# Two exponential buffers, pre-added sums from the sixth pair on, and a new order for an attention and gated-layer kernel

## The chip, the cores and the metric

The kernel runs on one core of a Trainium2 chip. Its time is microseconds of device time for one execution; the number compared is the median of several runs. Engines are named as the profile names them: PE (TensorE, matrix products), DVE (VectorE), ACT (ScalarE), POOL (GpSimd), SP (SyncE, which issues most DMAs). PEld is PE's weight load.

## What is computed

Causal attention with a bias from a running sum, then a gated layer, all in float32, on 8 batches of 8 heads, 576 positions and head size 64; the gated layer has width 1024.

```python
scores = scale * np.matmul(q, k.transpose(0, 1, 3, 2))
causal = np.triu(np.ones((S, S), dtype=bool), k=1)
s_pos = np.maximum(s, 0.0)
cum = np.cumsum(s_pos, axis=-1)
bias = -(cum[:, :, :, None] - cum[:, :, None, :])
scores = np.where(causal, -1000000000.0, scores + np.minimum(bias, 0.0))
scores = scores - np.max(scores, axis=-1, keepdims=True)
attn = np.exp(scores)
attn = attn / (np.sum(attn, axis=-1, keepdims=True) + 1e-09)
x = np.matmul(attn, v)           # then heads side by side: (B, S, 512)
...
h = np.maximum(x @ w_in, 0.0)
for k in range(3):               # along positions, zero padded
    conv_out += conv_w[k][None, None, :] * hp[:, k:k + S, :]
gate = 1.0 / (1.0 + np.exp(-conv_out))
return (h * gate @ w_out).astype(np.float32)
```

## The kernel before

**Work.** The 64 heads are 32 pairs; pair `p` holds two heads of batch `p // 4` on the two halves of the 128 partitions. Products are made to float32 accuracy from high and low parts (three products for one). Each pair goes through these steps (names in quotes are the task names in the code):

- "qk", "v": DMAs bring K, Q and V. "hi", "lo" split K and Q.
- "sh", "mx", "tn", "rt", "ds": rough scores on PE and their row maxima on DVE, turned and sent by DMA into a row that shifts the scores.
- "sc" (L1215 to L1234): the scores on PE, keys on partitions, four PSUM parts per pair. Pairs below `B0 = 9` get their causal mask as extra products from the tiles `mrow` and `unit`; later pairs get it on POOL ("mk", L1257).
- "ex" (L1248): ACT writes the exponentials into the tile `pt`, which holds both heads. There is one such tile, so a pair's exponentials come after the last reader of the pair before.
- "ad" (L1296): from pair 9 on, four additions fold the five key blocks of `pt` into the tile `ad` (all but the first 128 columns). Each may run on DVE or on POOL. The mask tiles `mrow` and `unit` lie in the memory of `ad`, so the first additions wait for the last mask products ("last_mask").
- "sum" (L1311): PE sums the exponentials over the keys, with `onehot` as weights; 28 products of a pair without additions, 10 with them. "pv" (L1273): PE multiplies the exponentials by V.
- "gd", "fo", "inv", "ri", "rb": ACT copies the sums, SP folds them over partitions (`rc`), DVE takes reciprocals (L1365), SP stores them in DRAM (L1370) and spreads them over the partitions of the one tile `rb` (L1380). "vn" copies the value product to `vc`, "nm" multiplies in place in `rb`, "xh" and "xl" (L1409, L1413) write the high and low parts of x in two position halves, into rings `x0` of 6 and `x1` of 8 slots.

A batch whose four pairs are done goes through the gated layer in two position halves: "h" (L1440, PE, groups of 24 products for two blocks of w_in), ACT's relu, the three taps on DVE and ACT, the sigmoid on ACT, the gate product on DVE, its high and low parts into ring `u`, and "o" (L1591, PE, groups of 12). Early on the weights are unpacked on ACT, POOL and DVE through staging tiles; the narrow pieces of w_out go through the tiles `ht` and `ct`.

**Order.** The order on each engine is fixed when the program is built. `Sched.play` is a planner: each task has the engines it may run on, a cost, the tasks and buffers it needs, and a due time from its place (`at(p)`, `h_tag`), shifted by a number of the table `DUE` for its kind and pair. It plays the program and always takes the ready task that is due first. Where PE has nothing ready for 0.6 us it puts in a fill product (`stay_awake`, L1668). The order it finds is then written out, and each engine runs its own list in that order, with semaphores for the true dependences.

Of the kernel before, what the change touches and what calls it, by code (L numbers as in the profile page):

```python
# [31 lines left out]
NX = (6, 8)  # L32
# [45 lines left out]
B0 = 9  # L78
RB = 7
# [16 lines left out]
    "pads":  # L96
        "0 -135.98 1 -136.71 2 -132.38",
    "ind":
# [398 lines left out]
def kernel(  # L497
# [91 lines left out]
    if RB < NP:  # L589
        EK_t.append(ep.tile([P, FW], F32R, name="eke"))  # L590
# [331 lines left out]
    for ch in range(2):  # L922
        for f in range(NF):
# [16 lines left out]
            if wide:  # L940
                t_wo[f, 1] = t_wo[f, 0]
                staged.append(t_wo[f, 0])
# [803 lines left out]
```

## Time and profile before

| | us |
|---|---|
| runs | 757.16, 758.41, 758.78 |
| median | 758.41 |
| profiled execution, its own time | 753.07 |
| its span, first to last instruction | 751.3 |
| mean granted TensorE clock in the span | 1.000 |

The profile has one row per instruction with start and duration. "Busy" is the time in which an engine has at least one instruction in work. A row of the timeline joins instructions of one line on one engine that follow each other; `x48` is their number. A product of float32 stands as two records where it is one row in the order with a count. Windows give busy time in a stretch of the span. Pairs are counted from 0, so the sixth pair is pair 5.

### The profile page before, as it was taken

What the parts mean: (1) busy time and instruction counts of PE and PEld (TensorE: products, weight loads), DVE (VectorE), ACT (ScalarE), POOL (GpSimd) and SP (SyncE); (2) the same over time, 40 slices, a digit from 0 to 9 for tenths busy, and PEclk for the clock granted to TensorE, in tenths of its full rate; (3) what the DMA queues carried; (4) which work ended last, traced back from release to release, by engine and by line L of the source; (5) the groups of instructions that cost most, each with busy time, mean ns of one, the idle gap of its engine ahead of it and who ended that gap; (6) DMA issues with size and microseconds to landing.
All of it is one profiled execution on the core that took longest, in us unless ns stands there. A gap on an engine that the chain in (4) does not pass through costs nothing.

```text
span 751.3 us, 24363 instructions
## 1 busy us (share of the span) xinstructions
PE 730.9 (97%) x10052; PEld 616.2 (82%) x10052; DVE 536.1 (71%) x1404; ACT 392.1 (52%) x676; POOL 335.2 (45%) x466
## 2 busy tenths in 40 slices
PE   8999999999999999999999999999999999999999
PEld 6777798888889887788887888887878877888897
DVE  7898987676888458678777468776856758655642
ACT  6557656365654346553646446474654436623531
POOL 6684445314436447544342547534664733410000
PEclk9999999999999999999999999999999999999999
DMA  7765631532323333342323433234222432010001
GB/s 224 222 193 156 200 100 38 161 102 83 114 72 93 115 97 102 102 126 68 97 69 112 130 116 99 83 93 152 83 68 64 135 102 64 19 43 20 29 30 44
DMA packets 50089, 75.50 MB, mean 100 GB/s; under 512 B 13690, under 2 KB 26298, under 8 KB 49978
## 3 DMA queue, kind: packets, MB, share of 16 engines
q1 hardware_dynamic: 49960, 73.92, 32.6%
q8 instruction: 79, 1.29, 0.7%
q14 instruction: 32, 0.26, 0.1%
q10 hardware_dynamic: 18, 0.02, 0.0%
HBM read 63.53 MB, written 10.03 MB: 98 GB/s over the span
## 4 chain that ended last, share of the span: by engine, by line
PE 45%; DVE 9%; issue 3%; ACT 2%; POOL 2%; DMA 1%; POOLq 0%; ACTq 0%; DVEq 0%; SPq 0%
PE ps L1448 15%; PE ps L1602 15%; PE ps L1232 7%; PE ps L1283 5%; DVE ps L1145 3%; DVE ct L1502 2%; PE ps L1335 1%; PE ps L1108 1%; DVE r L1145 1%; DVE ct L1523 1%; PE ps L1668 1%; DMA rw<-cum_d 1%; DVE ct L1486 1%; ACT pt L1249 0%; POOL ad L1298 0%
## 5 line engine op out<-in xcount | busy, mean ns | idle before, releaser
L1448 PE MATMUL ps<-x,wi 64*128 64x258 f32 (+1 forms) x3072 | 227.1, 297 | 5.4 <-DVE ct L1523 3.9
L1448 PEld LDWEIGHTS ps<-x,wi 64*128 64x128 f32 x3072 | 212.5, 186 | 12.5 <-DVE ct L1523 5.5
L1602 PE MATMUL ps<-wo,u 64*128 64x512 f32 x1536 | 196.9, 394 | 0.9
L1602 PEld LDWEIGHTS ps<-wo,u 64*128 64x128 f32 x1536 | 140.3, 185 | 28.7 <-ACTq L813 3.2
L1145 DVE CUSTOM_DVE_ANT_0 ps<-ps,rw 128x448 f32<-128x448 f32 (+4 forms) x250 | 109.5, 439 | 46.1 <-POOL rw L1066 17.4
L1249 ACT ACTIVATE pt<-ps,less 128x1024 f32<-128x1024 f32 (+1 forms) x128 | 116.1, 928 | 41.8 <-PE ps L1232 36.1
L1502 DVE SCALAR_TENSOR_TENSOR ct<-ps,cw_sb,ct 128x255 f32<-128x255 f32 (+3 forms) x256 | 115.9, 507 | 2.8 <-ACT ct L1484 2.7
L1232 PE MATMUL ps<-s 64*128 64x288 f32 (+4 forms) x1152 | 106.8, 299 | 2.8 <-DVE ct L1523 1.3
L1066 POOL TENSOR_SCALAR_AFFINE_SELECT rw<-rw 128x256 f32<-128x256 f32 (+1 forms) x125 | 47.7, 390 | 111.9 <-DVE r L1145 43.6
L1283 PE MATMUL ps<-pt,v 128*32 128x448 f32 (+4 forms) x1536 | 92.8, 388 | 0.0
L1232 PEld LDWEIGHTS ps<-s 64*128 64x128 f32 (+1 forms) x1152 | 81.1, 177 | 9.3 <-ACT pt L1249 2.6
L1283 PEld LDWEIGHTS ps<-pt,v 128*32 128x32 f32 x1536 | 50.6, 110 | 39.8 <-issue 29.9
L1260 POOL TENSOR_SCALAR_AFFINE_SELECT pt<-pt 128x256 f32<-128x256 f32 (+1 forms) x115 | 42.8, 390 | 88.9 <-ACT pt L1249 60.4
L1469 ACT ACTIVATE ps<-ps 128x642 f32<-128x642 f32 (+1 forms) x64 | 40.8, 637 | 71.5 <-PE ps L1448 67.9
L1517 ACT ACTIVATE ct<-ct 128x640 f32<-128x640 f32 (+1 forms) x64 | 43.8, 685 | 62.3 <-DVE ct L1502 59.4
L1523 DVE TENSOR_TENSOR ct<-ct,ps 128x640 f32<-128x640 f32 (+1 forms) x64 | 48.0, 751 | 18.6 <-ACT ct L1517 18.5
L1537 POOL TENSOR_TENSOR u<-ct,u 128x512 fp32r<-128x512 f32 x32 | 41.3, 1290 | 44.4 <-ACT u L1532 39.7
L1486 DVE TENSOR_SCALAR ct<-ps,cw_sb 128x256 f32<-128x256 f32 (+1 forms) x52 | 26.1, 513 | 47.6 <-ACT ct L1484 39.8
L1413 POOL TENSOR_TENSOR x<-rb,x 128x322 fp32r<-128x322 f32 (+1 forms) x50 | 37.7, 776 | 47.1 <-ACT x L1409 43.0
L1108 PE MATMUL ps<-s 64*128 64x288 f32 (+4 forms) x384 | 47.8, 307 | 5.2 <-ACT pt L1249 1.6
L1532 ACT CAST u<-ct 128x512 fp32r<-128x512 f32 x59 | 36.5, 618 | 25.8 <-DVE ct L1523 24.4
L1232 PE MATMUL ps<-eq,ek 64*128 64x288 f32 (+1 forms) x360 | 49.8, 297 | 0.0
(121 smaller groups left out, 980.2 us busy)
## 6 DMA issues: line engine op xcount, KB each, us to landing
raw<-qk SPq DMA_DIRECT2D x32, 576.0 KB
rw<-cum_d SPq DMA_DIRECT2D x25, 576.0 KB
v<-vp SPq DMA_DIRECT2D x32, 320.0 KB
rb<-ri_d SPq DMA_DIRECT2D x64, 144.0 KB
out<-ob SPq DMA_DIRECT2D x32, 256.0 KB
w<-w_in SPq DMA_DIRECT2D x8, 512.0 KB
ht<-w_out SPq DMA_DIRECT2D x8, 256.0 KB
w<-w_out SPq DMA_DIRECT2D x4, 512.0 KB
```

Of the source, the lines that this page charges most:

```text
L1066: nc.gpsimd.affine_select(out=RW_t[:, :, o : o + k], in_=RW_t[:, :, d : d + k], pattern=[[0, 2], [-1, k]], compare_op=ALU.is_ge, fill=NEG, ...
L1108: nc.tensor.matmul(dst[j], l, m, start=(k == 0), stop=(k == 1 or late))
L1145: nc.vector.tensor_tensor_reduce(out=bank(pb, j, o, o + c1 - c0), in0=bank(pb, j, o, o + c1 - c0), in1=add_, scale=1.0, scalar=acc if c0 e ...
L1232: nc.tensor.matmul(d, l, m, start=(k < 2), stop=(k >= len(steps) - 2 or (t == L and k < 2)), skip_group_check=t == L,)
L1249: nc.scalar.activation(PT[:, :, o : o + w], both(pb, 0, w), AF.Sigmoid, bias=less, scale=0.125,)
L1260: nc.gpsimd.affine_select(out=reg, in_=reg, pattern=[[0, 2], [1, dg]], compare_op=ALU.is_ge, fill=0.0, base=0, channel_multiplier=-1,)
L1283: nc.tensor.matmul(bank(pvs, n, o0, o0 + c1 - c0)[gs], vt[0:jt, t, gs], PT_t[g // 2][0:jt, O_T[t] + c0 : O_T[t] + c1], start=(t == 0), sto ...
L1448: mm = nc.tensor.matmul(bank(hb, i, 0, XW[hf]), wi[rows[j], k_ // 2, c, f * P : f * P + P], x[rows[j]], start=not turned and k == 0, stop= ...
L1502: nc.vector.scalar_tensor_tensor(cc[:, lo:hi], h_[:, sh + lo : sh + hi], cw_sb[:, 3 * f + k : 3 * f + k + 1], cc[:, lo:hi], op0=ALU.mult, ...
L1517: nc.scalar.activation(cc, cc, AF.Sigmoid)
L1523: nc.vector.tensor_tensor(cc, cc, both(hb, 2 * hf, 2 * hf + hw), op=ALU.mult)
L1602: mm = nc.tensor.matmul(bank(pb2 if m else pb, m, 0, cw_), l, r, start=turned + fp + n == 0, stop=turned == 1 and fp == FP - 1 and n == le ...
```

## The change

There are two tiles `pt`; each holds both heads of a pair and is given to a pair as a whole. Additions on `ad` start at pair 5 (`AD0`) instead of 9 (`B0`, which still rules the masks), so pairs 5 to 8 make ten sum products instead of 28 and sixteen additions more are made. `mrow` and `unit` have tiles of their own, and the first additions no longer wait for the last mask products. To make room, `x1` has 6 slots instead of 8, `rt` one instead of two, and the staging tiles `ht` lie in the memory that is given up when the gated layer's tiles are opened; all pieces of w_out (`staged`) and `cw` must be done before that. All numbers of `DUE` are new, so every engine's order is new.

```diff
-NX = (6, 8)
+NX = (6, 6)
...
 B0 = 9
+AD0 = 5
 RB = 7
...
-        "s -485.52 clear -169.14 ident -54.42 tab 40.83 hot -2.04 unit 129.42 mrow 278 "
+        "s -447.43 clear -126.39 ident -67.62 tab 470.29 hot 614.44 unit 108.55 mrow -399.5 "
...
-    PT = const.tile([P, 2, sum(W_T)], F32, name="pt")
-    PT_t = [PT[:, j] for j in range(2)]
+    PT_t = [const.tile([P, 2, sum(W_T)], F32, name=f"pt{i}") for i in range(NPT)]
...
-    mrow = ad_t.bitcast(BF16).rearrange("p a c -> p (a c)")[:, 0 : 4 * P].rearrange(
-        "p (k i m) -> p k i m", k=2, i=2
-    )
-    unit = ad_t.bitcast(BF16).rearrange("p a c -> p (a c)")[:, 4 * P : 4 * P + D]
+    mrow = const.tile([P, 2, 2, P], BF16, name="mrow")
+    unit = const.tile([P, D], BF16, name="unit")
...
-    RT_t = [const.tile([2 * NT, P], F32R, name=f"rt{i}") for i in range(2)]
+    RT_t = [const.tile([2 * NT, P], F32R, name=f"rt{i}") for i in range(1)]
...
-    H_t = [const.tile([P, 2, XW[0]], F32, name=f"ht{i}") for i in range(NHT)]
...
+    H_t = [ep.tile([P, 4 * P], F32, name=f"ht{i}") for i in range(NHT)]
...
-                staged.append(t_wo[f, 0])
+            staged.append(t_wo[f, ch])
...
-        ad = buf("ad") if p >= B0 else None
+        ad = buf("ad") if p >= AD0 else None
...
                     tt_on(e)(
-                        acc, PT[:, :, P:S] if t == 1 else acc,
-                        PT[:, :, O_T[t] : O_T[t] + W_T[t]], op=ALU.add,
+                        acc, PT_t[pts[0].slot][:, :, P:S] if t == 1 else acc,
+                        PT_t[pts[0].slot][:, :, O_T[t] : O_T[t] + W_T[t]], op=ALU.add,
                     )
...
-                    [m for t_, m in masks if t_ in (t - (t == 1), t)] + [t_ad] + last_mask, A + 2, pre_add,
+                    [m for t_, m in masks if t_ in (t - (t == 1), t)] + [t_ad], A + 2, pre_add,
...
-    stage_left = set(t_wi.values()) | set(staged) | set(last_sh)
+    stage_left = {t_cw} | set(t_wi.values()) | set(staged) | set(last_sh)
```

The order on PE, first eight of the fourteen rows of pair 5's sums before (`ps` is PSUM; the columns of a product stand last):

```order
L1335 MATMUL ps_64<-pt,onehot 32x144 x8
L1335 MATMUL ps_64<-pt,onehot 32x16
L1335 MATMUL ps_64<-pt,onehot 32x144 x3
L1335 MATMUL ps_64<-pt,onehot 32x16
L1335 MATMUL ps_64<-pt,onehot 32x144 x3
L1335 MATMUL ps_64<-pt,onehot 32x32
L1335 MATMUL ps_64<-pt,onehot 32x144 x2
L1335 MATMUL ps_64<-pt,onehot 32x32
```

The same place in the new order, the second head's sums and the value product behind them:

```order
L1336 MATMUL ps_66<-pt_89,onehot 32x128
L1336 MATMUL ps_66<-ad,onehot 32x16
L1336 MATMUL ps_66<-ad,onehot 32x144 x3
L1284 MATMUL ps_66<-pt_89,v_87 32x128 x4
L1284 MATMUL ps_66<-pt_89,v_87 32x448 x8
L1284 MATMUL ps_66<-pt_89,v_87 32x320 x4
L1284 MATMUL ps_66<-pt_89,v_87 32x192 x4
L1284 MATMUL ps_66<-pt_89,v_87 32x64 x4
```

Three rows, five products, stand for each head; the exponentials come from the second of the two `pt` tiles, and most columns from `ad`.

PE behind the last pair's value product (its last row is the first one here), before; `x_90` is the ring `x1`, L1448 the hidden layer, L1602 the output:

```order
L1283 MATMUL ps_65<-pt,v_87 32x64 x4
L1448 MATMUL ps_64<-x_90,wi 128x258 x24
L1448 MATMUL ps_65<-x_90,wi 128x258 x24
L1602 MATMUL ps_66<-wo,u_1699 128x512 x12
L1448 MATMUL ps_65<-x_90,wi 128x258 x24
L1602 MATMUL ps_66<-wo,u_1700 128x512 x12
L1448 MATMUL ps_64<-x_90,wi 128x258 x24
L1602 MATMUL ps_66<-wo,u_1701 128x512 x12
```

And in the new order, where `x_91` is the ring `x1`:

```order
L1284 MATMUL ps_67<-pt_88,v_87 32x64 x4
L1449 MATMUL ps_64<-x_91,wi 128x258 x24
L1603 MATMUL ps_65<-wo,u_1777 128x512 x12
L1449 MATMUL ps_64<-x_91,wi 128x258 x24
L1603 MATMUL ps_65<-wo,u_1778 128x512 x12
L1603 MATMUL ps_65<-wo,u_1779 128x512 x12
L1669 LDWEIGHTS mask
L1669 MATMUL ps_66<-mask 128x256
```

Two hidden-layer groups, both of batch 6, are left instead of five with 258 columns; behind the last row shown follow 22 more fill products, two output groups and then the first products that need x of pair 31.

DVE in the same place, from the copy of the last pair's value product on, before:

```order
L1389 COPY vc<-ps_65 128x128
L1389 COPY vc<-ps_65 128x448
L1486 TENSOR_SCALAR ct_103<-ps_64,cw_sb 128x256
L1502 SCALAR_TENSOR_TENSOR ct_103<-ps_64,cw_sb,ct_103 128x256 x2
L1365 RECIPROCAL rc<-rc 128x9
L1502 SCALAR_TENSOR_TENSOR ct_103<-ps_64,cw_sb,ct_103 128x255 x2
L1523 TENSOR_TENSOR ct_103<-ct_103,ps_64 128x2x256
```

And in the new order:

```order
L1390 COPY vc<-ps_67 128x128
L1390 COPY vc<-ps_67 128x448
L1366 RECIPROCAL rc<-rc 128x9
L1410 CAST x_90<-rb 128x322
L1410 CAST x_91<-rb 128x258
L1414 TENSOR_TENSOR x_90<-rb,x_90 128x322
L1414 TENSOR_TENSOR x_91<-rb,x_91 128x258
L1503 SCALAR_TENSOR_TENSOR ct_102<-ps_64,cw_sb,ct_102 128x256 x2
L1503 SCALAR_TENSOR_TENSOR ct_102<-ps_64,cw_sb,ct_102 128x255 x2
L1524 TENSOR_TENSOR ct_102<-ct_102,ps_64 128x2x256
L1538 TENSOR_TENSOR u_1775<-ct_102,u_1775 128x512
L1393 TENSOR_TENSOR rb<-vc,rb 128x576
```

The casts and subtractions of x of pair 30 now stand behind pair 31's reciprocal; before they stood ahead of the first row shown (the casts on ACT).

## Rows read from the trace of the kernel before

**Rows 1.** The page's busy times: us (share of the span) xinstructions, by engine.

```profile
PE 730.9 (97%) x10052; PEld 616.2 (82%) x10052; DVE 536.1 (71%) x1404; ACT 392.1 (52%) x676; POOL 335.2 (45%) x466
```

**Rows 2.** Windows of four stretches: length, busy time by engine, PEclk, DMA share, GB/s.

```profile
0.00:108.00 108.00, 102.58 (x1580) 81.25 (x1582) 94.06 (x203) 67.15 (x118) 65.36 (x71) 1.00 0.64 188
108.00:250.00 142.00, 139.73 (x2028) 121.71 (x2026) 106.11 (x298) 74.43 (x126) 57.17 (x82) 1.00 0.31 95
250.00:666.00 416.00, 405.47 (x5487) 340.95 (x5487) 293.47 (x816) 219.34 (x378) 209.43 (x310) 1.00 0.31 94
666.00:752.00 86.00, 83.16 (x973) 72.33 (x965) 42.50 (x88) 31.22 (x55) 3.24 (x4) 1.00 0.10 33
```

**Rows 3.** The same windows for the fill products of L1668 alone.

```profile
0.00:108.00 108.00, 23.85 (x164) 16.19 (x164) 1.00 0.64 188
250.00:666.00 416.00, 3.03 (x23) 2.01 (x23) 1.00 0.31 94
666.00:752.00 86.00, 5.17 (x41) 3.69 (x41) 1.00 0.10 33
```

**Rows 4.** PE's timeline, sums and value product of pairs 4 and 9: start, us, what.

```profile
84.08 1.77 PE L1335 MATMUL ps<-pt,onehot 128*32 128x144 f32 x54
85.72 2.87 PE L1283 MATMUL ps<-pt,v 128*32 128x128 f32 x46
...
192.81 0.30 PE L1335 MATMUL ps<-pt,onehot 128*32 128x128 f32 x1
193.38 2.87 PE L1283 MATMUL ps<-pt,v 128*32 128x128 f32 x48
```

**Rows 5.** Tile ad: ns min/median/max, first and last start; then L1413 from the lines.

```profile
L1298 POOL TENSOR_TENSOR ad<-ad,pt x37: 448/1007/1570, 187.9 to 660.2; 128x128 f32<-128x128 f32 x15, 128x384 f32<-128x384 f32 x13, 128x640 f32<-128x640 f32 x9
L1298 DVE TENSOR_TENSOR ad<-ad,pt x32: 278/573/2356, 205.8 to 661.3; 128x640 f32<-128x640 f32 x14, 128x384 f32<-128x384 f32 x10, 128x128 f32<-128x128 f32 x8
L1298 POOL TENSOR_TENSOR ad<-pt x16: 2102/2118/2128, 179.0 to 637.1; 128x896 f32<-128x896 f32 x16
L1298 DVE TENSOR_TENSOR ad<-pt x7: 1079/1086/1150, 203.0 to 656.5; 128x896 f32<-128x896 f32 x7
...
L1413 DVE TENSOR_TENSOR x<-rb,x 128x322 fp32r<-128x322 f32 (+1 forms) x14 | 7.1, 545 | 1.4 <-PE ps L1448 1.1 <-ACT x L1409 0.2
```

**Rows 6.** PE's timeline, the sums of pairs 19 and 20 and their value products.

```profile
421.37 0.30 PE L1335 MATMUL ps<-pt,onehot 128*32 128x128 f32 x1
422.66 2.87 PE L1283 MATMUL ps<-pt,v 128*32 128x128 f32 x48
...
437.59 0.30 PE L1335 MATMUL ps<-pt,onehot 128*32 128x128 f32 x1
...
439.25 2.87 PE L1283 MATMUL ps<-pt,v 128*32 128x128 f32 x48
```

**Rows 7.** Timelines of PE, SP and POOL behind the last pair's value product.

```profile
666.48 3.18 PE L1448 MATMUL ps<-x,wi 64*128 64x258 f32 x48
670.86 1.63 PE L1448 MATMUL ps<-x,wi 64*128 64x258 f32 x24
672.32 1.55 PE L1602 MATMUL ps<-wo,u 64*128 64x512 f32 x12
673.69 1.62 PE L1448 MATMUL ps<-x,wi 64*128 64x258 f32 x24
...
672.31 1.17 SPq L1380 DMA_DIRECT2D rb<-ri_d  x2
...
679.62 1.49 POOL L1413 TENSOR_TENSOR x<-rb,x 128x322 fp32r<-128x322 f32 x2 [18.40 <-ACT x L1409]
```

**Rows 8.** POOL's timeline, the low part of x of pair 20.

```profile
466.27 1.49 POOL L1413 TENSOR_TENSOR x<-rb,x 128x322 fp32r<-128x322 f32 x2 [2.98 <-DVE rc L1365]
```

**Rows 9.** Tile wo, the staging's last step on POOL: ns min/median/max, first and last start.

```profile
L934 POOL TENSOR_TENSOR wo<-ct,wo x5: 733/739/831, 66.9 to 105.8; 128x256 fp32r<-128x256 f32 x5
```

More of the change, by code (lines that the diff above doesn't have):

```diff
@@ L91 @@
     "x":
[4 rows of a table removed]
[4 rows of a table added]
     "pads":
-        "0 -135.98 1 -136.71 2 -132.38",
+        "0 35.97 1 144.1 2 512.86",
     "ind":
[1 row of a table removed]
[1 row of a table added]
     "cw":
[1 row of a table removed]
[1 row of a table added]
     "wi":
[3 rows of a table removed]
[3 rows of a table added]
     "wo":
[6 rows of a table removed]
[6 rows of a table added]
     "qk":
[9 rows of a table removed]
[9 rows of a table added]
     "hi":
[4 rows of a table removed]
[4 rows of a table added]
     "lo":
[4 rows of a table removed]
[4 rows of a table added]
     "dr":
[4 rows of a table removed]
[4 rows of a table added]
     "dp":
[1 row of a table removed]
[1 row of a table added]
     "dq":
[1 row of a table removed]
[1 row of a table added]
     "eq":
[4 rows of a table removed]
[4 rows of a table added]
     "sh":
[4 rows of a table removed]
[4 rows of a table added]
     "tn":
[4 rows of a table removed]
[4 rows of a table added]
     "sc":
[4 rows of a table removed]
[4 rows of a table added]
     "pv":
[4 rows of a table removed]
[4 rows of a table added]
     "nm":
[4 rows of a table removed]
[4 rows of a table added]
     "fo":
[4 rows of a table removed]
[4 rows of a table added]
     "vn":
[4 rows of a table removed]
[4 rows of a table added]
     "rw":
[3 rows of a table removed]
[4 rows of a table added]
     "rk":
[14 rows of a table removed]
[16 rows of a table added]
 }
@@ L588 @@
     EB_t = ep.tile([P, FW], F32R, name="eb")
+    H_t = [ep.tile([P, 4 * P], F32, name=f"ht{i}") for i in range(NHT)]
     if RB < NP:
         EK_t.append(ep.tile([P, FW], F32R, name="eke"))
-    s_sb, ones = PT[0:NH, 1, 0:S], PT[0:NH, 1, S : 2 * S]
-    cum, grid, rest_sb = PT[0:NH, 0, 0:S], PT[0:NH, 0, S : 2 * S], ones
+    s_sb, ones = PT_t[-1][0:NH, 1, 0:S], PT_t[-1][0:NH, 1, S : 2 * S]
+    cum, grid, rest_sb = PT_t[-1][0:NH, 0, 0:S], PT_t[-1][0:NH, 0, S : 2 * S], ones
     scratch = V_t[1].rearrange("p t c -> p (t c)")
@@ L620 @@
     pools = {
-        "raw": Pool(NR), "s": Pool(NS), "ek": Pool(NE), "eke": Pool(1), "eq": Pool(NEQ), "v": Pool(2), "pt": Pool(1), "x0": Pool(NX[0]), "x1": Pool(NX[1]),
-        "rb": Pool(1), "ad": Pool(1), "r8": Pool(2), "rt": Pool(2), "ri": Pool(1), "rw": Pool(1), "u": Pool(NRING), "us": Pool(1),
+        "raw": Pool(NR), "s": Pool(NS), "ek": Pool(NE), "eke": Pool(1), "eq": Pool(NEQ), "v": Pool(2), "pt": Pool(NPT), "x0": Pool(NX[0]), "x1": Pool(NX[1]),
+        "rb": Pool(1), "ad": Pool(1), "r8": Pool(2), "rt": Pool(1), "ri": Pool(1), "rw": Pool(1), "u": Pool(NRING), "us": Pool(1),
         "ht": Pool(NHT), "ct": Pool(NHT), "ob": Pool(NOB), "vc": Pool(1), "qsh": Pool(2), "qsc": Pool(2), "qh": Pool(2), "qo": Pool(1),
@@ L833, in parts @@
                 return wd.bitcast(U32).rearrange("p (c t) -> p c t", t=2), wb.bitcast(U32)
-            wd = H_t[wd_.slot].rearrange("p a c -> p (a c)")[:, 0 : 2 * n].bitcast(U32)
+            wd = H_t[wd_.slot][:, 0 : 2 * n].bitcast(U32)
             wc = C_t[wc_.slot].rearrange("p a c -> p (a c)")
@@ L1249, in sc_exp @@
                 nc.scalar.activation(
-                    PT[:, :, o : o + w], both(pb, 0, w), AF.Sigmoid, bias=less, scale=0.125,
+                    PT_t[pts[0].slot][:, :, o : o + w], both(pb, 0, w), AF.Sigmoid, bias=less, scale=0.125,
                 )
@@ L1258, in sc_mask @@
                     jt, dg = J_T[t], min(P, W_T[t])
-                    reg = PT[0:jt, :, O_T[t] : O_T[t] + dg]
+                    reg = PT_t[pts[0].slot][0:jt, :, O_T[t] : O_T[t] + dg]
                     nc.gpsimd.affine_select(
@@ L1284, in run @@
                                 bank(pvs, n, o0, o0 + c1 - c0)[gs], vt[0:jt, t, gs],
-                                PT_t[g // 2][0:jt, O_T[t] + c0 : O_T[t] + c1],
+                                PT_t[pts[0].slot][0:jt, g // 2, O_T[t] + c0 : O_T[t] + c1],
                                 start=(t == 0), stop=(n == 0 or t == NT - 1),
@@ L1314, in sums @@
             for j in range(2):
-                pt = PT_t[j]
+                pt = PT_t[pts[0].slot][:, j]
                 if ad:
```

167 rows, old and new, of the table DUE are left out of this document.

## The prediction

> **What bounds the kernel now.** I read the page's busy times first. TensorE (PE) is busy for 97% of the span of 751.3 us, the next engine, VectorE (DVE), for 71% [rows 1]. The windows by stretch then show where PE is not busy: 5.4 us of the first 108, 2.3 of the next 142, 10.5 of the 416 up to the last pair's value product, 2.8 at the end [rows 2]. The reader should see two more things there: DVE is busy for 94.06 of the first 108 us, the only stretch in which another engine is near its limit, and the granted clock is 1.00 (2.4 GHz) in all four. The same windows for L1668 alone give the fill products, which keep PE at work while it has nothing to do: 164 + 23 + 41 of them in three of the four stretches, 23.85 + 3.03 + 5.17 = 32.05 us of PE's busy time, so 0.145, 0.13 and 0.126 us each [rows 3]. So the time is PE's real products, plus fill, plus some 20 us of waits. A change counts as far as it alters one of these three. What it gives to DVE or POOL counts only where PE then waits.
>
> **The change, part by part.** My sum stands against the profiled execution, 753.07 us (span 751.3, 1.8 outside it). The median of the three runs is 758.41, 5.3 higher; I take the difference over to it unchanged.
>
> *Sums of four pairs.* A pair without pre-additions has 28 products in the order and 56 records in the trace. They run from 84.08 until the value product has PE to itself at 85.72, which is 1.64 us with two of its records inside, so about 1.62. With pre-additions there are 10 products, from 192.81 to 193.38, 0.57 us [rows 4]. The new order has the ten in pairs 5 to 8 too. PE's products are otherwise the same in number. That is 4 x 1.05 = **-4.2 us**, all on PE, and PE is the bound.
>
> *The additions that pay for it.* Sixteen more on `ad`. Over the whole program the order gives POOL 71 instead of 53 of them, and DVE 37 instead of 39. By the rows the POOL part is one more of 2.1 us and 17 more of about 1.0, some 19 us [rows 5]. In exchange DVE does the low part of x for 14 pairs instead of 7, 14 instructions more at 0.545, 7.6 us [rows 5]. Cost on PE: 0. What covers it: POOL is idle for 85 and DVE for 36 of the 142 us after 108, where pairs 6 to 8 come, and DVE for 123 of the next 416 [rows 2]. Pair 5's additions fall at the edge of the first stretch. If that cover is gone and DVE does all four (1.1 and three of about 0.57) while it bounds, it is +2.8. I take 0, because a bound below 0 has no reason and the second buffer gives the additions more time.
>
> *Second buffer of exponentials.* Before, the exponentials of a pair wait until the previous pair's value product has read the one buffer, and the additions and the sums queue behind them. Two sums show it: 421.37 to 422.66 and 437.59 to 439.25, 1.29 and 1.66 us in place of 0.57, together 1.8 us of waiting for additions [rows 6]. In the new order scores of the next pair often stand ahead of a pair's sums, so additions get a lead. Between 0 and -1.8 I take the middle, **-0.9**, since a new order can be late in another place.
>
> *Fill.* Counted by row, the order has 156 before the first hidden-layer product instead of 164, 1 instead of 23 in the middle, and 70 instead of 41 behind the last sums, 32 of these behind the last output product in both. At the prices above: -8 x 0.145 - 22 x 0.13 + 29 x 0.126 = **-0.4**. The gain of the middle is thus nearly all given back at the end.
>
> *The end, where the smaller ring acts.* `x1` goes from 8 slots to 6. A batch holds 4, so the third and fourth pair of a batch can't be written before the second half of the batch before is done. The DVE piece shows it: pair 30's casts of x now stand behind pair 31's reciprocal. The chain of the last pair, from its value product at 666.48 over sums, reciprocal, two trips to DRAM (the second issued at 672.31) and x to the low part, which starts at 679.62 and takes 1.49, is 14.6 us long; PE had other products meanwhile [rows 7]. In the new order PE has until it needs x of pair 31: two hidden-layer groups of 1.46, five output groups of 1.38 (the lengths are the steps of [rows 7]: 670.86 to 672.32, and 672.32 to 673.69), and 23 fill products, 2.9 + 6.9 + 2.9 = 12.7 us. `x1` is free 1.46 + 1.38 + 1.46 = 4.3 us after the value product; pair 30's two casts (some 0.3 each, an estimate from half of a subtraction) and two subtractions (0.545) end at 6.0, and only then may the reciprocals come back into `rb`, 5.8 us after the value product before. SP has nothing else queued between the two trips. So the chain is about 14.9 and PE waits **+2.2**. The bounds are 0 (less traffic on DVE and ACT there than in the trace) and +11, if the chain is as long as pair 20's: 439.25 + 2.87 to 466.27 + 1.49 is 25.6 us [rows 6, 8].
>
> *No price:* mask rows in memory of their own and one `rt` instead of two. The staging of the narrow pieces of w_out must now end before the tiles `u` open; the last one that POOL wrote was at 105.8 [rows 9], about where the new order has the last of them, ahead of the first write to `u`.
>
> Sum: -4.2 - 0.9 - 0.4 + 2.2 = **-3.3 us**: 749.8 for a profiled execution, **755.1** for the median of runs.
>
> **Rivals.**
> *More is gained.* The second buffer also shortens waits that carry no name of its own. Of the 10.5 us that PE is not busy between 250 and 666 [rows 2], half go: -3.3 - 5.2 = -8.5, 749.9. For it: the middle of the new order holds one fill product. Against it: DVE is busy for 71% of that stretch and gets more work.
>
> *The port: no change.* In the trace one addition on DVE took 2.356 us where the median is 0.573 [rows 5]. Suppose DVE stands still for half of POOL's 19 us more, 9.5 us, and a third of that reaches PE: +3.2, the sum is about 0, 758.3. Against it: the median of DVE's additions is far below the one long one, and DVE has idle time in both stretches where they fall. The Trainium skill speaks against the change here: "SBUF — State Buffer", section "Who interferes with whom", says that a DVE instruction with both inputs in SBUF contends with a GpSimd instruction that reads SBUF, and that the later one is blocked until the other is through. The one long addition fits that rule and the medians do not show it as the usual case.
>
> *The last chain is long: slower.* One mechanism, after the last value product. If the chain there takes 25.6 us like pair 20's, PE waits 25.9 - 12.7 = 13.2 instead of 2.2, and the sum is +7.7, 766.1. It decides at a chain of 14.9 + 3.3 = 18.2 us; from 19.7 on the kernel is slower by more than 0.2%. For it: pair 20. Against it: the DMA share is 0.10 there against 0.31 in the middle [rows 2], and the last chain of before was 14.6.
>
> *The change is not what it says:* the order has pairs that write either buffer, so I give this nothing.
>
> **How the numbers follow.** The forecast's own band, -7 to -1.5 us, has 0.46; more gained 0.15; no change (by the port, or waits elsewhere that eat the 3.3) 0.16; slower 0.23, of it 0.14 for the last chain and 0.09 for DVE in the first 108 us and for waits the new order makes that I can't see. A measurement of this kernel can tell some 0.2% (1.5 us) from no change, so faster is 0.61, same 0.16, slower 0.23. The range goes down to 747.5 (-10.9: the first rival with all 1.8 us of the sums' waits and a little of the end) and up to 762.0 (+3.6: a last chain of some 22 us, or pair 5's additions and the port together); about 2 in 10 lie outside.
>
> **What would show it.** Sums of pairs 5 to 8 at 0.57 us; no sums above 0.8 after pair 9; fill products 1 in the middle and 70 at the end; POOL's `ad` group up by about 19 us with DVE's medians unchanged; a PE gap of 1 to 4 us before the first hidden-layer product of the last batch. I am wrong if DVE's additions get longer than their medians as a rule, if PE is busy for less than 405 of the 416 us in the middle, or if the gap before the last batch is over 6 us.

## The result, and the profile after

The changed kernel takes **764.93 us** (median of 7 runs, 763.41 to 770.81) beside 758.45 for the kernel before on the same chip: a ratio of 1.0103, 95% interval 1.0077 to 1.0129, so 1% slower. The forecast was 755.1 us, 3.3 less than before; 764.93 lies outside its range of 747.5 to 762.0. The slower runs of a kernel have the lower mean granted clock (19 runs of the kernel before: 754.1 to 754.6 us at 1.000, 758.0 to 759.5 at 0.995), and the profiled execution of before is a fast one, so that the spans here differ by more than the medians. It has no stretch at half TensorE clock before its last 2 us, the one after has three.

The page after, to be held beside [rows 1]: busy times.

```profile
span 763.1 us, 24054 instructions
PE 729.5 (96%) x9907; PEld 612.9 (80%) x9907; DVE 552.9 (72%) x1433; ACT 391.5 (51%) x679; POOL 333.5 (44%) x456
```

The span grew by 11.8 us and TensorE's busy time fell by 1.4. So PE stands idle 13.2 us longer. The windows by stretch, with the bounds moved to the same places of the program as in [rows 2], say where:

```profile
0.00:122.00 122.00, 111.44 (x1619) 87.78 (x1621) 100.52 (x206) 74.59 (x126) 63.44 (x64) 0.94 0.56 167
122.00:265.00 143.00, 136.70 (x1878) 115.33 (x1876) 105.04 (x299) 76.11 (x136) 61.41 (x89) 0.99 0.31 95
265.00:682.00 417.00, 402.94 (x5535) 342.15 (x5531) 310.62 (x853) 215.59 (x376) 202.64 (x298) 1.00 0.31 94
682.00:764.00 82.00, 78.44 (x886) 67.69 (x886) 36.68 (x78) 25.23 (x45) 6.00 (x6) 1.00 0.09 28
```

PE is not busy for 10.6, 6.3 and 14.1 us where it was 5.4, 2.3 and 10.5, and at the end for 3.6 instead of 2.8. And the granted clock of the first stretch is 0.94 where it was 1.00. The first hidden-layer product shows the same from another side. Of the two groups of these products the first is before's, the second after's (min/median/max ns, first and last start):

```profile
L1448 PE MATMUL ps<-x,wi x3072: 273/303/417, 95.0 to 732.6; 64*128 64x322 f32 x97, 64*128 64x258 f32 x95
```

```profile
L1449 PE MATMUL ps<-x,wi x3072: 273/303/416, 104.7 to 741.8; 64*128 64x322 f32 x96, 64*128 64x258 f32 x96
```

It starts 9.7 us later, and the last one 9.2 us later: most of the loss is there before the gated layer begins.

**The first place.** After's timelines of ACT, POOL, DVE and PE from 62 to 69 us (start, us, what; in brackets the idle time before and what ended it):

```profile
63.14 0.43 ACT L853 ACTIVATE ct<-ht 128x256 f32<-128x256 f32 x1 [4.00 <-DMA ht<-w_out]
...
63.66 0.84 POOL L857 TENSOR_SCALAR ct<-ct 128x256 f32<-128x256 f32 x1 [2.27 <-ACT ct L853]
...
64.53 0.29 DVE L863 TENSOR_SCALAR ct<-ct 128x256 uint32<-128x256 uint32 x1 [1.26 <-POOL ct L857]
...
65.34 2.48 DVE L1126 TENSOR_REDUCE r<-ps 128x2 f32<-128x896 f32 x4
...
66.68 1.49 PE L1233 MATMUL ps<-s 64*128 64x448 f32 x6 [2.21 <-DVE r L1126]
```

This is a chain of queues. A narrow piece of w_out lands late; ACT, POOL and DVE each hold an instruction for it at the head of their queue. DVE's four maxima stand behind it, though their data is there, and PE needs the bank that they read, for the product that starts at 66.68.

**The second place.** POOL and DVE, then PE, from 84 to 90 us:

```profile
84.81 2.86 POOL L995 TENSOR_TENSOR s<-raw,s 128x1152 fp32r<-128x1152 f32 x1 [1.70 <-ACT s L989]
...
85.12 3.17 DVE L1393 TENSOR_TENSOR rb<-vc,rb 128x576 f32<-128x576 f32 x1
...
89.13 1.03 PE L1669 MATMUL ps<-mask 128*128 128x256 bf16 x8 [3.31 <-ACT vc L1390]
```

DVE's norm takes 3.17 us, the longest of 32 with a median of 0.754. It begins 0.3 us after a subtraction on POOL and ends 0.6 us after it, as if it had only begun when POOL was through. That is the rule that the prediction cited from the Trainium skill ("SBUF — State Buffer", section "Who interferes with whom"): the later of the two is blocked until the other is through. This trace agrees, but on instructions that the prediction had not looked at. Only then can ACT copy `vc`, and PE waits 3.3 us for the bank.

**What follows both.** Windows of 2 us, the column before the last two is the granted clock:

```profile
64.00:66.00 2.00, 0.47 (x8) 0.23 (x4) 1.47 (x3) 1.01 (x3) 0.50 (x1) 1.00 0.93 316
66.00:68.00 2.00, 1.32 (x8) 0.87 (x10) 2.00 (x5) 0.00 (x0) 0.00 (x0) 0.55 0.47 164
68.00:70.00 2.00, 2.00 (x26) 1.86 (x24) 1.31 (x5) 0.67 (x1) 0.00 (x0) 0.50 0.66 168
70.00:72.00 2.00, 2.00 (x23) 1.65 (x20) 0.73 (x3) 1.51 (x3) 1.86 (x2) 0.50 0.79 244
72.00:74.00 2.00, 2.00 (x15) 1.45 (x15) 1.92 (x2) 2.00 (x4) 0.87 (x1) 0.75 0.16 39
...
86.00:88.00 2.00, 0.00 (x0) 0.00 (x0) 2.00 (x1) 0.00 (x0) 1.68 (x1) 1.00 0.25 97
88.00:90.00 2.00, 0.87 (x8) 0.68 (x7) 2.00 (x4) 1.62 (x5) 0.48 (x1) 1.00 0.00 0
90.00:92.00 2.00, 1.82 (x11) 0.96 (x9) 1.55 (x6) 1.78 (x5) 2.00 (x3) 0.52 0.28 16
92.00:94.00 2.00, 2.00 (x22) 1.70 (x22) 1.06 (x3) 1.32 (x3) 2.00 (x3) 0.50 0.58 191
...
96.00:98.00 2.00, 2.00 (x53) 1.70 (x49) 2.00 (x7) 0.62 (x1) 0.00 (x0) 0.77 0.04 11
```

PE was busy 0.47 of the 2 us in one place and 0.87 of 4 in the other, and behind each the clock goes from 2.4 to 1.2 GHz for some 7 us. Such a wait is paid twice: once while it lasts, once in the products after it.

**What came as forecast.** The sums of pairs 5 to 31 all take 0.57 us. Pair 6's in PE's timeline, to be held beside [rows 4]:

```profile
129.90 0.30 PE L1336 MATMUL ps<-pt,onehot 128*32 128x128 f32 x1
...
130.47 0.39 PE L1284 MATMUL ps<-pt,v 128*32 128x128 f32 x8
```

The additions, beside [rows 5]:

```profile
L1299 POOL TENSOR_TENSOR ad<-ad,pt x54: 457/1019/1597, 119.9 to 672.3; 128x384 f32<-128x384 f32 x19, 128x640 f32<-128x640 f32 x19, 128x128 f32<-128x128 f32 x16
L1299 DVE TENSOR_TENSOR ad<-ad,pt x27: 277/547/849, 106.1 to 673.4; 128x128 f32<-128x128 f32 x11, 128x640 f32<-128x640 f32 x8, 128x384 f32<-128x384 f32 x8
L1299 POOL TENSOR_TENSOR ad<-pt x17: 2139/2157/2183, 116.8 to 666.7; 128x896 f32<-128x896 f32 x17
```

The long one of 2.356 us is gone. At the end PE does not wait for x of pair 31: the products behind the last value product follow each other, and DVE's last step on that x is done before PE's first product that needs it, at 695.33.

```profile
681.93 1.72 PE L1449 MATMUL ps<-x,wi 64*128 64x258 f32 x24
...
689.13 2.68 PE L1669 MATMUL ps<-mask 128*128 128x256 bf16 x23
691.80 3.69 PE L1603 MATMUL ps<-wo,u 64*128 64x512 f32 x24
695.33 5.94 PE L1449 MATMUL ps<-x,wi 64*128 64x322 f32 x78
...
693.86 0.83 DVE L1414 TENSOR_TENSOR x<-rb,x 128x322 fp32r<-128x322 f32 x2 [0.73 <-PE ps L1603]
```

### The profile page after: what moved, and what is told of

The parts are those of the page before. It is cut to its first block, busy times and chain, and to the rows that moved or that the text cites. A ratio compares the mean times of both kernels' runs of the same rounds, so it can differ in the third digit from the quotient of the medians.

```text
span 763.1 us, 24054 instructions
## 1 busy us (share of the span) xinstructions
PE 729.5 (96%) x9907; PEld 612.9 (80%) x9907; DVE 552.9 (72%) x1433; ACT 391.5 (51%) x679; POOL 333.5 (44%) x456
## 5 line engine op out<-in xcount | busy, mean ns | idle before, releaser
L1250 ACT ACTIVATE pt<-ps,less 128x576 f32<-128x576 f32 (+1 forms) x128 | 116.8, 926 | 48.1 <-PE ps L1233 47.3
L1146 DVE CUSTOM_DVE_ANT_0 ps<-ps,rw 128x64 f32<-128x64 f32 (+4 forms) x250 | 109.6, 439 | 42.8 <-POOL rw L1067 19.7
L1503 DVE SCALAR_TENSOR_TENSOR ct<-ps,cw_sb,ct 128x320 f32<-128x320 f32 (+3 forms) x256 | 116.3, 508 | 2.5 <-ACT ct L1485 2.1
L1233 PE MATMUL ps<-s 64*128 64x288 f32 (+4 forms) x1152 | 110.2, 304 | 8.1 <-DVE r L1126 3.0
L1233 PEld LDWEIGHTS ps<-s 64*128 64x128 f32 (+1 forms) x1152 | 83.4, 181 | 15.5 <-ACT pt L1250 3.8
L1284 PEld LDWEIGHTS ps<-pt,v 128*32 128x32 f32 x1536 | 48.6, 110 | 41.8 <-issue 31.0
L1487 DVE TENSOR_SCALAR ct<-ps,cw_sb 128x320 f32<-128x320 f32 (+1 forms) x52 | 26.4, 517 | 55.3 <-ACT ct L1485 50.9
L1299 POOL TENSOR_TENSOR ad<-ad,pt 128x384 f32<-128x384 f32 (+2 forms) x54 | 56.6, 1047 | 14.5 <-DVE ad L1299 10.1
L1109 PE MATMUL ps<-s 64*128 64x288 f32 (+4 forms) x384 | 49.4, 315 | 7.7 <-DVE r L1146 6.3
L1109 PEld LDWEIGHTS ps<-s 64*128 64x128 f32 x384 | 33.3, 189 | 19.3 <-DVE r L1146 11.1
```

The lines of the kernel that those rows point to most:

```text
L1109: nc.tensor.matmul(dst[j], l, m, start=(k == 0), stop=(k == 1 or late))
L1146: nc.vector.tensor_tensor_reduce(out=bank(pb, j, o, o + c1 - c0), in0=bank(pb, j, o, o + c1 - c0), in1=add_, scale=1.0, scalar=acc if c0 e ...
L1233: nc.tensor.matmul(d, l, m, start=(k < 2), stop=(k >= len(steps) - 2 or (t == L and k < 2)), skip_group_check=t == L,)
L1250: nc.scalar.activation(PT_t[pts[0].slot][:, :, o : o + w], both(pb, 0, w), AF.Sigmoid, bias=less, scale=0.125,)
L1284: nc.tensor.matmul(bank(pvs, n, o0, o0 + c1 - c0)[gs], vt[0:jt, t, gs], PT_t[pts[0].slot][0:jt, g // 2, O_T[t] + c0 : O_T[t] + c1], start= ...
L1299: tt_on(e)(acc, PT_t[pts[0].slot][:, :, P:S] if t == 1 else acc, PT_t[pts[0].slot][:, :, O_T[t] : O_T[t] + W_T[t]], op=ALU.add,)
```

## The experiments

Theory 1: the new order costs the time, by waits like the two above. Theory 2: the additions do, through DVE and POOL. Twelve kernels ran. A thirteenth, the changed kernel with the old table of numbers, has no result: the planner stops at 740 us of its own time with the work of pair 6 still undone, so new structure and new numbers were not measured apart. The order here is a list that the planner makes; most of the experiments edit this list after it is made, so that all else stays in place. `to_after(names, last)` takes the named steps out of the list and puts them behind the step `last`.

**The two places mended.** In the changed kernel:

```diff
+    to_after(["wo0.0q", "wo0.0m", "wo0.01"], "mx4.1.0")
+    named["lo6.0"].after = named["nm2"]
```

The first line puts ACT's, POOL's and DVE's steps on the late piece behind the four maxima. The second makes POOL's subtraction wait until the norm is through.

> The changed kernel with two places of its early order mended: the three steps of the narrow w_out piece whose transfer lands late (ScalarE L853, POOL L857, VectorE L863) go behind the work that waited for them, and POOL's subtraction L995 of the seventh pair waits for VectorE's L1393 beside which it ran. Theory 1: the TensorE gaps at 64 to 66 and 86 to 88 us go, with them both half-clock stretches of the first 100 us, and 5 to 10 us come back: 755 to 760, the first h product at 96 to 99 us. Rival (the two gaps are symptoms, VectorE and POOL are behind anyway): under 3 us come back, 762 or more, other gaps in their place before 105 us.

Measured: 759.05 us, ratio to before 1.0038 (1.0014 to 1.0061) instead of 1.0103: of a loss of 1.03%, 0.65% is back, 4.9 us, just under the 5 to 10 of theory 1. The norm beside its neighbour now, DVE and POOL:

```profile
82.36 0.75 DVE L1393 TENSOR_TENSOR rb<-vc,rb 128x576 f32<-128x576 f32 x1
...
83.24 2.96 POOL L995 TENSOR_TENSOR s<-raw,s 128x1152 fp32r<-128x1152 f32 x1 [2.88 <-DMA ek<-grid_d]
```

In its profiled execution both half-clock stretches are gone, and the first hidden-layer product starts at 96.6 us, 1.6 later than in the kernel before. Same instructions, four places in queues: theory 1 holds for the early stage. That also speaks against the smaller rings and the earlier end of the staging as the cause there, since both are still in this kernel. The loss that is left, 0.38% or 2.9 us, is not explained.

**The first place alone.** The first of the two lines.

> The changed kernel with the first of the two places alone mended (the narrow w_out piece whose transfer lands late). Theory 1 (two separate waits, each followed by its own half-clock stretch): 3 to 4.5 us back against the changed kernel, the stretch at 66 us gone and the one near 90 us still there at its place in the program: 760 to 762. Rival (the second follows from the first): 757 to 760, as with both mended.

Measured: 762.70 us, 1.0061 (1.0029 to 1.0093): 0.42 of the 0.65% is back, 3.2 us, but its interval overlaps those of the changed kernel and of the one with both mended. Pair 3's sums, at 74.43 us in the changed kernel, start 4.2 us sooner, and the second wait is still there with its stretch (windows of 6 us, granted clock 0.69 and 0.50):

```profile
82.00:88.00 6.00, 3.64 (x21) 2.29 (x20) 5.24 (x8) 3.21 (x7) 3.56 (x4) 0.69 0.27 97
88.00:94.00 6.00, 6.00 (x76) 4.60 (x76) 4.48 (x11) 1.61 (x5) 2.93 (x3) 0.50 0.55 148
```

So the second wait does not follow from the first, as theory 1 had it.

**A wait planted in the kernel before.** Five maxima over the constant mask, results unused, at two places in DVE's queue.

```diff
+            for _ in range(5):
+                nc.vector.tensor_reduce(out=spare, in_=mask, axis=mybir.AxisListType.X, op=ALU.max)
+    for t in order:
+        if t.name in ("mx4.3.0", "ad12.3"):
+            held_up(t)
```

> The kernel before, with five maxima over the constant mask (about 0.5 us each on VectorE, results unused) planted at two places: before the last four maxima of the fifth pair, near 63 us, and before the third addition of the 13th pair, near 240 us. Theory 1 (a wait of TensorE of about 2 us costs itself and more, as the clock falls to half behind it): each costs 2 to 5 us, together 5 to 9, 762 to 766, with the granted clock at half in a stretch behind at least one of them. Rival (a wait costs only itself, or VectorE catches up): together under 5 us, the granted clock stays at 1.0.

Measured: 764.99 us, 1.0106 (1.0073 to 1.0139). The plant's row on DVE, and the windows behind it:

```profile
68.68 3.22 DVE L1692 TENSOR_REDUCE spare<-mask 128x1 f32<-128x448 bf16 x5
```

```profile
68.00:74.00 6.00, 3.33 (x54) 2.62 (x53) 5.86 (x10) 3.11 (x6) 3.58 (x5) 1.00 0.46 154
74.00:80.00 6.00, 6.00 (x98) 4.41 (x100) 6.00 (x15) 3.23 (x5) 0.00 (x0) 0.72 0.36 53
```

The kernel before has PE at 6.00 and 5.89 of these 6 us. Lined up by PE's rows the first plant costs 4.3 us, with half clock behind it, and the second 2.5 us without; by the ratio both cost 8.0. So 3.2 us on DVE, at a place where PE needs what DVE hands on, costs 2.5 to 4.3: DVE does not catch up. One late step of this size costs about as much as the whole forecast gain of 3.3.

**The additions dropped.** On the kernel with both places mended: the 16 additions of pairs 5 to 8 are taken out of the list and their sums go over five tiles again.

```diff
+    order = [t for t in order if not re.match("ad[5-8][.]", t.name)]
...
-                if ad:
+                if p >= B0:
```

> The kernel of the two mended waits, its order kept word for word, but with the 16 additions of pairs 5 to 8 left out of it and the sums of these four pairs taken over all five tiles as before. Theory 1 (the sums were priced rightly, the additions are covered): four sums of 1.62 in place of 0.57 us, so 4 us more than the kernel of the two mended waits, 762 to 764. Theory 2 (the additions hinder the other work on VectorE and POOL): the same as that kernel or less, 756 to 759, since what the longer sums cost comes back between them.

Measured: 764.92 us, 1.0095 (1.0057 to 1.0133) against 1.0038 (1.0014 to 1.0061): 0.57% or 4.3 us more. The four sums were priced at 4.2. No time comes back without the additions, so theory 2 falls for this kernel. But the traces don't bear out that the sums alone cost the 4.3. The spans differ by 5.1 us, and 3.6 of them are there when pair 4's value product starts, ahead of the first addition that was dropped (96.8 us with the additions). The value product with and without them, and the windows before it, with and without:

```profile
89.25 0.30 PE L1284 MATMUL ps<-pt,v 128*32 128x128 f32 x2
...
92.80 0.30 PE L1284 MATMUL ps<-pt,v 128*32 128x128 f32 x2
```

```profile
82.00:92.00 10.00, 8.92 (x158) 6.62 (x156) 9.80 (x22) 5.44 (x12) 8.20 (x6) 1.00 0.50 148
...
82.00:92.00 10.00, 9.39 (x90) 6.56 (x91) 7.73 (x17) 4.72 (x10) 7.88 (x6) 0.52 0.45 141
```

The kernel without additions is at half clock there, in a place that the edit leaves as it was; why is not known. From pair 4's to pair 8's value product it loses 3.2 us more, of which 1.6 are left at the end. So on these traces the sums with their additions are worth 1.6 to 3.2 us of time.

**The additions in the old order.** The kernel before, its list kept; mask rows and unit column get memory of their own, the additions are put into the queues behind the exponentials that they read, and the sums go behind the value product so that the additions lie beside it.

```diff
+        order.insert(next(i for i, x in enumerate(order) if x.start >= at), n)
...
+        last = max(i for i, x in enumerate(order) if x.name == f"pv{p}" or x.name == f"ad{p}.4")
+        order.insert(last + 1, s_)
```

> The kernel before with its order kept, and only the sums of pairs 5 to 8 changed: mask rows and unit column in memory of their own, the first addition of each of these pairs put into POOL's queue and the other three into VectorE's, each right behind the work that the order has up to the exponentials it reads, and the product with v of these pairs ahead of their sums, so that the additions lie beside it. Theory 1 (the sums are worth what was forecast, the changed kernel loses by its order): 3 to 4.5 us under the kernel before. Theory 2 (the additions hinder other work as much as the sums save): within 1 us of it or over, with a TensorE gap of over 1 us within 15 us of one of the additions.

> As the kernel with the sums of pairs 5 to 8 changed in the old order, but for pairs 6 to 8 alone, so that no addition falls into the first 105 us, where VectorE still stages the weights. Theory 1: 2.3 to 3.4 us under the kernel before; 1 us more than with the fifth pair, unless the additions of pair 5 stop TensorE in the staging stage: then less than with it. Theory 2: within 1 us of before.

Measured: 768.94 us, 1.0173 (1.0142 to 1.0204), and with pairs 6 to 8 alone 766.54 us, 1.0149 (1.0118 to 1.0180). Theory 1 missed by 16 and 14 us. The kernel with three sums shows one reason, on DVE and POOL:

```profile
131.09 3.26 DVE L1299 TENSOR_TENSOR ad<-ad,pt 128x640 f32<-128x640 f32 x1 [0.44 <-POOL ad L1299]
...
131.03 2.64 POOL L994 TENSOR_TENSOR s<-raw,s 128x1152 fp32r<-128x1152 f32 x1
```

An addition of 0.82 us takes 3.26 beside POOL's subtraction: the same collision, now with an addition.

**The additions in turn, and the moved sums alone.** Two controls. In the first all twelve additions are on DVE and the subtraction that collided follows them (`lo8.0` behind `ad6.4`). In the second only the sums move behind the value product, without additions.

> As the kernel with three sums changed in the old order, but all twelve additions of pairs 6 to 8 in VectorE's queue, and POOL's subtraction L994 that ran beside the sixth pair's addition (which took 3.26 us there, 0.82 elsewhere) put behind the last of that pair's additions. Theory 4 (the additions cost what they stretch beside POOL's work, and nothing where they take turns): 3 us of the three sums come back, 1 to 3.3 us under the kernel before. Theory 5 (VectorE has no room left at these places in the old order: 2.7 us of additions a pair move the maxima behind them, for which TensorE waits): 3 to 9 us over the kernel before, with all additions of 1.09, 0.82, 0.55 and 0.28 us.

> The kernel before with nothing changed but the place of three sums: in pairs 6 to 8 the product with v goes ahead of the sums, as in the two kernels with additions in the old order; the sums are over five tiles and there are no additions. If the additions made those kernels slow: within 1 us of the kernel before. If the later sums did (the reciprocal and the norm start 1.6 us later instead of the product with v): 3 to 10 us over it.

Measured: 765.82 us, 1.0114 (1.0090 to 1.0137), and 757.20 us, 0.9999 (0.9977 to 1.0022). The moved sums cost nothing. The additions take 1.1, 0.8, 0.6 and 0.3 us almost throughout, and still the kernel is 8.6 us slower than with the sums moved alone, though the shorter sums are worth 3.1. But the collision is not gone. The subtraction that was put behind the additions now runs beside the gate product, which takes 0.69 us in the kernel with the sums moved alone. DVE and POOL:

```profile
136.01 2.98 DVE L1541 TENSOR_TENSOR u<-ct,u 128x512 fp32r<-128x512 f32 x1
...
135.79 2.66 POOL L994 TENSOR_TENSOR s<-raw,s 128x1152 fp32r<-128x1152 f32 x1 [5.89 <-issue]
```

PE's longest waits from 128 to 182 us (us in total, times, longest):

```profile
PE ps L1108 <- DVE r L1145: 1.8, 1, 1.8
PE ps L1232 <- DVE vc L1393: 1.3, 1, 1.3
PE ps L1232 <- DVE r L1145: 1.0, 1, 1.0
```

The waits for `vc` (1.3, until 139.9 us) and for the maxima of L1232 (1.0, until 141.8) come behind that product, the one of 1.8 us, until 154.5, behind pair 7's additions. Behind them the granted clock is 0.70 from 140 to 145 us and 0.66 from 155 to 160. The time is where theory 5 put it, and theory 4's forecast missed; but as a collision was left, the control does not part the two. That DVE is idle for 36 of 142 us does not make additions free in an order laid without them. Whether they are covered in the new order because the planner left room for them there, or by its second exponential buffer, was not tried.

**A third place.** From 215 us on the trace after shows another such stretch, still there with the two places mended. Windows of 5 us of that kernel:

```profile
210.00:215.00 5.00, 4.57 (x72) 3.56 (x66) 0.75 (x4) 1.97 (x5) 0.00 (x0) 1.00 0.59 182
215.00:220.00 5.00, 4.17 (x66) 3.76 (x64) 3.99 (x17) 0.19 (x1) 1.06 (x3) 1.00 0.32 113
220.00:225.00 5.00, 3.56 (x52) 3.02 (x48) 4.25 (x15) 4.20 (x9) 1.22 (x3) 1.00 0.34 108
...
230.00:235.00 5.00, 2.71 (x26) 2.19 (x24) 4.86 (x17) 3.62 (x7) 4.15 (x6) 0.85 0.36 118
```

DVE has 0.75 us of work in the 5 us in which the one buffer of mask rows, `rw`, is filled again, then too much, and PE waits for its maxima. In the kernel before DVE never has less than 3.2 of 5 us between 185 and 235 us. Two edits try to feed DVE sooner: first the last maxima of pair 10 go forward, so that `rw` is fetched 2.7 us sooner, then a scores product goes ahead of a hidden-layer product too.

```diff
+    to_after(["rk10.2"], "mx10.1.3.0")
+    to_after(["mx10.0.2.0", "mx10.1.2.0"], "tb1.1.1")
...
+    to_after(["rk10.1"], "mx10.1.2.0")
+    to_after(["mx10.0.1.0", "mx10.1.1.0"], "nm8")
...
+    to_after(["h1.1.4"], "sh11.2")
```

> The kernel of the two mended waits, with a third place mended: around the tenth pair's last maxima, POOL's cuts L1067 and VectorE's maxima L1146 of that pair go ahead of the subtraction L995, the norm's low part L1414 and the gate's product L1538 that stood before them, so that the one rw buffer comes free sooner and the next rows are fetched up to 3 us earlier than at 218.8 us. Theory 1 (the order's waits cost the time): of the 7 us lost between 215 and 247 us, 3 to 7 come back, with the half-clock stretch at 240 us gone: 752 to 756, under the kernel before. Rival (VectorE simply has too much work there): under 1.5 us, 757.5 to 760, TensorE still waits for the maxima.

> The kernel with the third place mended, and one PE move more: the 11th unit's h product of 258 columns (the second of the two that stand ahead of pair 11's third scores product L1109) goes behind that product, so that VectorE, which stands with little to do from 210 to 214 us there and has too much from 220 us on, gets the next maxima 1.5 us sooner. Theory 1 (TensorE's waits between 215 and 235 us come from VectorE being fed too late, then all at once): 1 to 2.5 us less than with the third place alone mended, 759 to 761.5, and the waits for maxima after it under 3 us in sum (4 us there). Rival (the work that follows sets the pace): within 1 us of the third place alone, 761.5 to 763.5, the same waits.

Measured: 762.27 us, 1.0072 (1.0045 to 1.0099), and with the second edit 760.04 us, 1.0048 (1.0021 to 1.0075). Neither beats the kernel with two places mended. The first edit is 2.6 us slower than that kernel, which neither forecast had. The second is 1.8 us under the first, in theory 1's range, and PE's waits for maxima between 200 and 245 us are 2.3 us instead of 3.0, as theory 1 had it; but the intervals overlap, so this is a hint. All of PE's named waits there are 4.8 us with two places mended, 4.9 with the first edit and 4.2 with both. After the first, DVE stands for 4 us at a step that waits for PE (L1182) in place of the rows. At pair 13's value product (283.38 us with two places mended, 283.11 and 282.27 with the edits) 0.3 and 1.1 us are won; the spans are 2.1 and 0.6 us longer all the same, with two more half-clock stretches, near 307 and 425 us. So the waits there can be shortened by a little, and what is won is lost further on. A second buffer for `rw` was not tried.

**Planned anew, two kernels that answer another question.** One part of the change alone in the kernel before (additions from the sixth pair on), and the changed kernel with additions from the tenth pair on. Both change one bound (in the second `AD0 = 9`; in the first also mask rows and unit column get memory of their own), and the planner lays the order anew from there with the same table of numbers.

```diff
-        ad = buf("ad") if p >= B0 else None
+        ad = buf("ad") if p >= AD0 else None
```

> The kernel before, with one part of the change alone: pre-added sums from the sixth pair on (mask rows and unit column in memory of their own, so that the buffer of the additions is free early). Buffers, x rings and the table of numbers are those of before. Theory 1 (the loss of the changed kernel comes from its order in the first 100 us and around 220 us): the sums of pairs 5 to 8 go from 1.62 to 0.57 us each and nothing else moves much, so 4 us less than before, 753 to 756. Theory 2 (the 16 more additions hinder POOL and VectorE): pairs 5 to 8 come no earlier, or the time is over 760; a TensorE gap of over 2 us next to one of the new additions.

> The changed kernel with the pre-added sums from the tenth pair on, as before: 16 additions fewer on POOL and VectorE, 32 sums of 1.62 instead of 0.57 us per four pairs. Its order is that of the changed kernel up to the sixth pair's additions. Theory 1: the first loss stays (it comes before the first addition at about 95 us), so +4 us against the changed kernel, 767 to 771, the two half-clock stretches at 66 and 90 us as they were. Theory 2: 762 or less, and the half-clock stretch at 240 us gone.

Measured: 789.50 us, 1.0429 (1.0388 to 1.0469), and 800.73 us, 1.0571 (1.0533 to 1.0608). In the first, theory 1 missed by 33 us, and the "over 760" of theory 2 is met by far more than it spoke of; in the second both missed, by 30 us and more. The order is another from pair 5's additions on, and the numbers, each of which shifts one step's turn, did not fit the new one. Whatever the additions do is drowned in that. It is why the others edit the finished list. One forecast for the second kernel came true: its first 100 us are those of the changed kernel, with the same two waits and half clock behind both (0.52 from 66 to 72 us, 0.51 from 90 to 96), ahead of any addition.

## Why the prediction was wrong

*Sums of four pairs, -4.2:* right on PE, 0.57 us each. When they were undone 4.3 us were lost, but the traces give only 1.6 to 3.2 of it to them, so that all of the 4.2 reaches the time is not shown.

*The additions, 0:* borne out in this order, as no time came back without them. The cover that was named, idle time of POOL and DVE, is no cover by itself: in the old order three pairs of additions cost 8.6 us more than the moved sums alone.

*Second buffer, -0.9; fill, -0.4; the end, +2.2:* the sums no longer wait for additions. The fills are 1 and 70 as counted, but 32.2 us in all instead of 32.05, so +0.15. The end was mis-sized: from the value product to the last step on x the chain takes 12.8 us (681.93 to 694.69) and not 14.9, and it was covered whole, so 0 instead of +2.2. The rival of the long last chain did not come about.

*"No price":* this is the step that failed. The prediction compared how many instructions of each kind there are and followed one place of the new order, the end. The waits of the new order stood in its sum at nothing, those in the staging of the first 108 us too, though it had written that DVE is busy for 94.06 of them. The new order's steps there make PE wait at two places, 2.2 and 3.3 us, with half clock behind both, and the four edited queue places give 4.9 us back. The prediction had 0.09 of the chance for DVE in the first 108 us and for "waits the new order makes that I can't see" together. Its rival of the port had the mechanism of the second place, but priced it on the additions. One of its signs of being wrong came true: in the middle PE is busy for 402.94 of 417 us, under the 405 of 416 that it had named.

Without the two waits the kernel would stand at 761.3 us by the ratio, inside the range. But they are not the whole of the miss. The terms as measured, with the sums at their full price, come to about -5 us (-4.2 - 0.9 + 0.15 + 0); with the two places mended the kernel is still 2.9 us over the one before. Some 8 us of the new order's cost thus have no cause shown, or 5 to 7 if the sums are worth only what the traces give them.

What is left can be read by busy time. With the two places mended the page says:

```profile
PE 725.2 (96%) x9907; PEld 609.5 (80%) x9907; DVE 549.7 (73%) x1433; ACT 392.2 (52%) x679; POOL 334.0 (44%) x456
```

That is 5.7 us less than before's 730.9, the sums among it, in a span 6.4 us longer (757.7), so 12.1 us more without work. Of these 2.4 lie in the first stretch, 4.5 in the second and 4.6 in the third, by the windows with the same bounds of the program. The largest of its named waits (us in total, times, longest) is this; the same row of the kernel before has 0.8 us in 2 times:

```profile
PE ps L1109 <- DVE r L1146: 6.7, 8, 1.6
```

PE waits for maxima: the order brings DVE its work in bursts. That the bursts cause the rest is argued from these rows; the one place where it was tried won about 1 us there and none in the end, and it stays open. Two rivals were not tried. The collision of the second place comes again in this kernel: the norm, 0.75 us as a rule, takes 1.69, 2.06 and 2.81 us beside POOL at 168, 471 and 521 us. And the six slots of `x1` and the single `rt` are in all the edited kernels with the new order.

## What to carry to other kernels

A change of order can't be priced by counting instructions. Walk each queue through the stage where a second engine is near its limit, and ask of each step that waits for a transfer which ready work stands behind it, and whose bank that work frees. Idle time on an engine is no cover by itself; and a table of numbers made for one order did not fit either of two edits that the planner saw.

## What the runs showed of the hardware

A DVE instruction on two inputs in SBUF took 3.17, 3.26 and 2.98 us instead of 0.75, 0.82 and 0.69 beside one on POOL that took 2.86, 2.64 and 2.66: it ended 0.5 to 0.7 us after POOL's, as if it had only then begun. Making POOL's wait for DVE's gave the 0.75 back; with the additions in turn, the subtraction that was moved behind an addition met the gate product instead.

With the two places mended the span is 5.4 us shorter; 4.3 of it is busy time of PE (729.5 to 725.2) for the same products, which run at 2.4 instead of 1.2 GHz in two stretches of some 7 us. PE's time without work fell by only 1.1 us, as shorter waits, without half clock behind them, took the place of the two (from 80 to 84 us PE is busy for 2.0 of 4 us).
